# A decode kernel whose output projection is summed in 20 + 6 + 4 + 2 rows instead of 24 + 5 + 3, and whose softmax sums and attention results are gathered for two batches at a time

## The chip, the cores and the metric

The kernel runs on one core of one Trainium2 chip. The metric is device time in microseconds (us) for one execution. The time before is the median of 3 runs, 200.6 us (200.33 to 200.7). One further execution was recorded by the hardware profiler; every duration below comes from that one.

## The reference, cut to what matters

One decoding step for 8 batches (B = 8), one query each, model width D = 512:

```python
xn = layernorm(x)                                     # 8 x 512
q  = xn @ wq                                          # 32 heads of 128
k, v = the last 2048 positions of k_cache, v_cache    # 8 kv heads, each shared by 4 query heads
p  = softmax(q . k * 128**-0.5)
o  = p . v                                            # 8 x 4096
s  = o @ wo                                           # wo: 4096 x 512
h  = sigmoid(xn @ w_gate) * (xn @ w_up)               # 8 x 1792
g  = silu(h @ w_down)
y  = x + s * g
```

Nearly all bytes are keys and values: 8 batches x 8 kv heads x 2048 positions x 128 numbers in bf16 is 32 MiB for the keys and as much for the values. wo has 4 MiB, wq 4 MiB, the three gate weights 5.25 MiB.

## The kernel before, in words

**Loads.** All large loads are issued by the SP queue, in one order that the program fixes with the list `todo` (`later`, `pump`, `free`, lines 107 to 132). A load is written into the program as soon as its pool has a free buffer: five buffers of 16 KiB a partition for keys (`kpool`), four for values (`vpool`). The order is x, the gate weights, wq, then for each batch and each half of its kv heads (`i` = 0, 1) one key transfer of 2 MiB and, three steps later, one value transfer of 2 MiB. At the end come the rows of wo, which use the key buffers. `load_rows` (line 97) lays wo out so that partition p holds rows 32p to 32p + 31 of it; "row t" below means the 128 x 512 slab of the t-th of these 32 rows over all partitions (128 KiB). Line 176 cuts the 32 slabs into four transfers of 14, 10, 5 and 3 rows.

**The loop over batches** (`for b in range(B)`) is written out by hand in 16 steps for each batch; each step turns half of a key chunk with TensorE (`k_transposes`, eight 128 x 128 transposes, copied out by VectorE at line 425) and then runs the tasks put into the step. For batch b these are its scores, the softmax of batch b-1 (`row_max`, `stat_rows`, `spread_max` on ScalarE, `p_transposes`), and the values of batch b-2 (`values`, `combine`). `sums(b)` (line 516) multiplies the row sums of the exponentials, one column `st[b]`, by a 0/1 matrix in fp32, so that each output row gets its softmax denominator, and VectorE takes the reciprocal into `inv[b]`. `combine(b)` (line 547) leaves batch b's unnormalised result in `o_sb`, 128 x 128. `normalise(b)` (line 565) gathers it by an fp32 matmul with the 0/1 matrix `sel_res`, multiplies by `inv[b]` on VectorE (line 574) and reduces it into bf16 columns of `oP_sb` (line 583), from which the output projection reads. In the loop `sums` is a task of step 13 and `normalise(b - 3)` one of step 0.

The one-bank PSUM tile `m_ps` holds all small results: the maxima, the denominators (`den_ps`) and the gathered results (`oR_ps`).

**The tail**, after the last batch's keys, is straight-line code from `scores(B - 1, NU - 1)` on. It ends the softmax of batches 6 and 7 and multiplies their values. The last value transfer (batch 7, second half) is used by `some(B - 1, 1, 0, CU)`; then come `combine(7)` and `normalise(7)`.

**The output projection.** The first KS = 24 rows go into `part_ps` (line 653): matmul t writes all 512 columns to the 32 partitions of column group j = t mod 4, so four rows run side by side. The four groups' sums have then to be added. `part_ps` is copied to SBUF, the left half by ScalarE (line 665), the right half by VectorE (line 666), and `into_blocks` (line 668) adds the four groups by an fp32 matmul with the 0/1 matrix `sel_z`. `into_blocks` cuts the 512 columns into four blocks of 128 that lie on the four groups of partitions, so it takes four matmuls for a row, side by side. The last 8 rows go straight through `into_blocks` to `fin_ps`. The order on TensorE is rows 24 to 28, then `sel_z` with the copies, then rows 29 to 31. Two VectorE operations (lines 693 and 695) multiply by the gate and add x, and two transfers, one from SP and one from ScalarE's queue, write the output.

Of the kernel before, what the change touches and what calls it, by code (L numbers as in the profile page):

```python
# [10 lines left out]
def kernel(  # L11
# [13 lines left out]
    nc = tc.nc  # L25
    P = 128
    B, _, D = A_x.shape
    _, Hkv, Sk, Dh = A_k_cache.shape
# [21 lines left out]
    f32 = mybir.dt.float32  # L50
    AF = mybir.ActivationFunctionType
    ALU = mybir.AluOpType
    AX = mybir.AxisListType
# [6 lines left out]
    ktpool = ctx.enter_context(tc.tile_pool(name="ktpool", bufs=3))  # L60
# [3 lines left out]
    small = ctx.enter_context(tc.tile_pool(name="small", bufs=2))  # L64
# [39 lines left out]
    weights = {}  # L104
# [27 lines left out]
        later(tag, f)  # L132

    RT = 32
    KS = 24

    x_bf = work.tile([B, D], bf16, name="x_bf")

# [2 lines left out]
    S = Z // B  # L141
# [29 lines left out]
    for n in range(len(order) + AHEAD):  # L171
        if n < len(order):
            want_cache(k_tiles, A_k_cache, "k", *order[n])
        if n >= AHEAD:
            want_cache(v_tiles, A_v_cache, "v", *order[n - AHEAD])
    for t0, t1 in ((0, 14), (14, KS), (KS, 29), (29, RT)):
        want_rows("wo_sb", A_wo, "k", RT, t0, t1)

    pump()
# [8 lines left out]
        out=perm[:].rearrange("k (l p) -> k l p", l=G),  # L188
        in_=ident[:].rearrange("k (p l) -> k l p", l=G),
# [13 lines left out]
        out=rstd[:], in_=mv[:, 1:2], func=AF.Sqrt, bias=eps_t[:], scale=1.0  # L203
# [4 lines left out]
        out=xn_bf[:],  # L208
        in0=x_f[:],
        scalar1=mv[:, 0:1],  # L210
        scalar2=rstd[:],
        op0=ALU.subtract,
        op1=ALU.mult,
# [3 lines left out]
    for kt in range(KT):  # L217
        nc.tensor.transpose(
            out=xnT_ps[:, kt, :],
            in_=xn_bf[:].rearrange("b (p kt) -> b kt p", kt=KT)[:, kt, :],  # L220
# [11 lines left out]
    for t in p_buf:  # L232
        nc.vector.memzero(t[:])
    oP_sb = work.tile([P, RT, Z], bf16, name="oP_sb")
    nc.vector.memzero(oP_sb[:])

    NDQ = Dh // RT
    own_q = consts.tile([P, NDQ], f32, name="own_q")
    nc.vector.reduce_sum(
        out=own_q[:], in_=ident_f[:].rearrange("k (h q) -> k q h", q=NDQ), axis=AX.X  # L240
    )
    sel_z = consts.tile([P, Z], f32, name="sel_z")
    nc.vector.reduce_sum(
        out=sel_z[:], in_=ident_f[:].rearrange("k (j z) -> k z j", z=Z), axis=AX.X
# [6 lines left out]
    def hidden(name):  # L251
# [21 lines left out]
        out=h_sb[:].rearrange("k t p -> k p t"),  # L273
        in0=sig[:, :FC].rearrange("k (p t) -> k p t", t=FT),
        in1=u_ps[:].rearrange("k (p t) -> k p t", t=FT),
# [5 lines left out]
        out=hT_sb[:].rearrange("k t z -> k (t z)"),  # L281
        in_=h_sb[:].rearrange("k t p -> k (t p)"),
# [4 lines left out]
    for t in range(FT):  # L287
        j = t % NB
# [3 lines left out]
            rhs=weights[("wd_sb", t)],  # L292
# [8 lines left out]
    for j in range(NB):  # L301
# [3 lines left out]
            rhs=w_sb[:, 0, j * P : (j + 1) * P],  # L305
# [15 lines left out]
    for kt in range(KT):  # L321
        for x in range(Hkv // JQ):
            for j in range(JQ):
# [4 lines left out]
                    rhs=weights[("wq_sb", kt)][:, g * rep * Dh : (g + 1) * rep * Dh],  # L328
# [13 lines left out]
    for x in range(Hkv // JQ):  # L342
        for r in range(rep):
            nc.tensor.transpose(
                out=qT_ps[:, x, r, :], in_=q_bf[:, x, r, :], identity=ident[:]
            )
        nc.vector.tensor_copy(
            out=qm_sb[:, :, x * JQ : (x + 1) * JQ, M0 : M0 + rep],
            in_=qT_ps[:, x].rearrange("d r (j z) -> d z j r", z=Z)[:, ::S],
# [50 lines left out]
    m_ps = ps_m.tile([P, 2, 256], f32, name="m_ps", tag="m")  # L400
    r_ps = [m_ps[0:1, x, 0:P] for x in range(2)]
    nb_ps = [m_ps[:, x, 0:1] for x in range(2)]
    den_ps = [m_ps[:, x, 1:2] for x in range(2)]
    oR_ps = [m_ps[:, x, P : 2 * P] for x in range(2)]

    kT = {}
    s_ps = {}
# [1 line left out]
    st = {}  # L409
    row = {}  # L410
    inv = {}

    def k_transposes(b, u, h):
        i, j = u // NJ, u % NJ
# [58 lines left out]
    def spread_max(b):  # L473
        nc.tensor.transpose(  # L474
            out=nb_ps[b % 2],
            in_=row.pop(b)[:].rearrange("o l j h -> o (l j h)"),
            identity=ident_f[0:1, 0:1],
        )
        nb = small.tile([P, 1], f32, name="nb")
        nc.scalar.copy(out=nb[:], in_=nb_ps[b % 2])  # L480

        s = s_ps.pop(b)
        st[b] = small.tile([P, 1], f32, name="sums")
        for l in range(G):
            rows = slice(NR * l, NR * (l + 1))
            nc.scalar.activation(  # L486
                out=p_buf[b % 2][rows, :, l, :],
                in_=s[rows, :].rearrange("k (c p) -> k p c", p=PG),
                func=AF.Exp,
                bias=nb[rows, :],  # L490
                scale=scale,
                accum_out=st[b][rows, :],
            )

    def p_transposes(b, h, copy=nc.vector.tensor_copy):
# [17 lines left out]
            )  # L513


    def sums(b):
        nc.tensor.matmul(
            den_ps[b % 2],
            lhsT=sel_sum[:].rearrange("k h q -> k (h q)"),
            rhs=st.pop(b)[:],  # L520
            start=True,
            stop=True,
        )
        inv[b] = small.tile([P, 1], f32, name="inv")
        nc.vector.reciprocal(out=inv[b][:], in_=den_ps[b % 2])


    def values(b, c, tiles=range(NQ)):
# [18 lines left out]
    def combine(b):  # L547
        del pT[b]
        o_odd = small.tile([P, Dh], f32, name="o_odd")
        nc.scalar.mul(  # L550
            out=o_odd[:], in_=o_ps[:, b % 2, Dh:], mul=own_col[:, 1:2]
        )
        o = small.tile([P, Dh], f32, name="o_sb")
        nc.vector.scalar_tensor_tensor(  # L554
            out=o[:],
            in0=o_ps[:, b % 2, :Dh],
            scalar=own_col[:, 0:1],
            in1=o_odd[:],
            op0=ALU.mult,
            op1=ALU.add,  # L560
        )
        row[b] = o


    def normalise(b):
        nc.tensor.matmul(  # L566
            oR_ps[b % 2],
            lhsT=sel_res[:].rearrange("k h q -> k (h q)"),
            rhs=row.pop(b)[:],
            start=True,  # L570
            stop=True,
        )
        own = small.tile([P, NDQ, RT], f32, name="own")
        nc.vector.scalar_tensor_tensor(  # L574
            out=own[:],
            in0=oR_ps[b % 2].rearrange("p (q t) -> p q t", q=NDQ),
            scalar=inv.pop(b)[:],
            in1=own_q[:].unsqueeze(2).to_broadcast([P, NDQ, RT]),
            op0=ALU.mult,
            op1=ALU.mult,  # L580
        )
        with nc.allow_low_precision(reason="one of the addends is not zero"):
            nc.vector.reduce_sum(
                out=oP_sb[:, :, S * b],
                in_=own[:].rearrange("p q t -> p t q"),
                axis=AX.X,
            )

    for b in range(B):
        pb = b - 1 if b >= 1 else None  # L590
        pp = b - 2 if b >= 2 else None
        tasks = {s: [] for s in range(2 * NU)}
        for u in range(NU - 1):
            tasks[2 * u + 3].append(lambda u=u: scores(b, u))
        if pb is not None:
            tasks[1].append(lambda: scores(pb, NU - 1))
            tasks[2].append(lambda: row_max(pb))
            tasks[4].append(lambda: stat_rows(pb))
            tasks[6].append(lambda: spread_max(pb))
            if b < B - 1:  # L600
                tasks[11].append(lambda: p_transposes(pb, 0))
                tasks[12].append(lambda: p_transposes(pb, 1))
                tasks[13].append(lambda: sums(pb))
        if pp is not None:
            for c in range(CU):
                tasks[1 + c // 3].append(lambda c=c: values(pp, c, (0,)))
                tasks[6 + c // 3].append(lambda c=c: values(pp, c, (1,)))
            tasks[13].append(lambda: combine(pp))
        if b >= 3:
            tasks[0].append(lambda: normalise(b - 3))  # L610
        for s in range(2 * NU):
            k_transposes(b, s // 2, s % 2)
            for f in tasks[s]:
                f()
# [10 lines left out]
    spread_max(B - 1)  # L625
    p_copy(B - 2, 1, nc.vector.tensor_copy)
    some(B - 2, 0, 0, CH)
    normalise(B - 3)
    sums(B - 2)
    some(B - 2, 0, CH, CU)  # L630
    some(B - 2, 1, 0, CH)
    p_turn(B - 1, 0)
# [3 lines left out]
    some(B - 2, 1, CH, CU)  # L636
    combine(B - 2)
    some(B - 1, 0, 0, CH)
    sums(B - 1)
    some(B - 1, 0, CH, CU)  # L640
    normalise(B - 2)
    some(B - 1, 1, 0, CU)
    combine(B - 1)
    normalise(B - 1)

    fin_ps = ps_s.tile([P, P], f32, name="fin_ps", tag="s")

# [3 lines left out]
    for t in range(KS):  # L651
# [7 lines left out]
            tile_position=(0, Z * j),  # L659
            skip_group_check=True,  # L660
        )
    part = [
        ktpool.tile([P, 2, D // 2], f32, name=f"part{x}", tag="kT") for x in range(2)
    ]
    nc.scalar.copy(out=part[0][:, 0, :], in_=part_ps[:, : D // 2])
    nc.vector.tensor_copy(out=part[1][:, 0, :], in_=part_ps[:, D // 2 :])

    def into_blocks(lhsT, rhs, start, stop):
        for j in range(NB):
            nc.tensor.matmul(  # L670
                fin_ps[Z * j : Z * (j + 1), :],
                lhsT=lhsT,
                rhs=rhs(j),
                start=start,
                stop=stop,
                tile_position=(0, Z * j),
                skip_group_check=True,
            )

    for t in range(KS, RT):  # L680
        if t == 29:
            into_blocks(
                sel_z[:],
                lambda j: part[j // 2][:, 0, (j % 2) * P : (j % 2 + 1) * P],
                False,
                False,
            )
        w = weights[("wo_sb", t)]
        into_blocks(
            oP_sb[:, t, :], lambda j: w[:, j * P : (j + 1) * P], t == KS, t == RT - 1  # L690
        )
    prod = work.tile([P, P], f32, name="prod")
    nc.vector.tensor_tensor(out=prod[:], in0=gg_sb[:], in1=fin_ps[:], op=ALU.mult)  # L693
    y_bf = work.tile([P, P], bf16, name="y_bf")
# [39 lines left out]
```

## Time and profile before

| what | value |
|---|---|
| median of 3 runs | 200.6 us (200.33 to 200.7) |
| the profiled execution's own time | 201.08 us |
| its span, first to last instruction | 198.9 us |
| outside the span (201.08 - 198.9) | 2.2 us |
| TensorE busy | 156.9 us (79%) |
| VectorE busy | 122.9 us (62%) |
| ScalarE busy | 37.4 us (19%) |
| moved by the DMA engines | 81.32 MB, 409 GB/s over the span |
| mean granted TensorE clock | 0.966 |

The profiled execution is 0.48 us above the median of the runs. In the profile, PE is TensorE's matmuls, PEld its weight loads, DVE is VectorE, ACT is ScalarE, and SPq the SP queue that issues transfers. A line of the timeline has the start in us, the duration in us, engine, line of the kernel, operation, output and inputs, shape and count; in brackets stands how long the engine had been idle before and what ended the wait. fp32 matmuls appear as two instructions each.

### The profile page before, as it was taken

What the parts mean: (1) busy time and instruction counts of PE and PEld (TensorE: products, weight loads), DVE (VectorE), ACT (ScalarE), POOL (GpSimd) and SP (SyncE); (2) the same over time, 40 slices, a digit from 0 to 9 for tenths busy, and PEclk for the clock granted to TensorE, in tenths of its full rate; (3) what the DMA queues carried; (4) which work ended last, traced back from release to release, by engine and by line L of the source; (5) the groups of instructions that cost most, each with busy time, mean ns of one, the idle gap of its engine ahead of it and who ended that gap; (6) DMA issues with size and microseconds to landing.
All of it is one profiled execution on the core that took longest, in us unless ns stands there. A gap on an engine that the chain in (4) does not pass through costs nothing.

```text
span 198.9 us, 4752 instructions
## 1 busy us (share of the span) xinstructions
PE 156.9 (79%) x2130; PEld 106.7 (54%) x2130; DVE 122.9 (62%) x230; ACT 37.4 (19%) x91; POOL 1.4 (1%) x10
## 2 busy tenths in 40 slices
PE   0434457999799996999898969998988698888652
PEld 0111126777676674667565646675656565566411
DVE  4724017899798584758874947587749575742301
ACT  4101010002601500060023000600230024082000
POOL 2000000000000000000000000000000000000000
PEclk9999999999999996999999978999999999999985
DMA  5999999999999999999999999999999999999960
GB/s 212 431 435 434 435 425 428 432 428 423 435 425 432 432 425 432 425 435 425 432 432 427 425 435 428 425 430 422 438 425 435 428 425 428 432 428 430 412 263 3
DMA packets 6155, 81.32 MB, mean 409 GB/s; under 512 B 752, under 2 KB 760, under 8 KB 1272
## 3 DMA queue, kind: packets, MB, share of 16 engines
q1 hardware_dynamic: 5938, 80.10, 94.4%
q10 hardware_dynamic: 198, 0.93, 1.3%
q8 instruction: 16, 0.26, 0.5%
q14 instruction: 3, 0.02, 0.0%
HBM read 81.02 MB, written 0.01 MB: 407 GB/s over the span
## 4 chain that ended last, share of the span: by engine, by line
DMA 75%; PE 22%; SPq 1%; issue 0%; DVE 0%
DMA k_sb<-in_A_k_cache_dram 61%; PE kT_ps L420 13%; DMA wo_sb<-in_A_wo_dram 11%; PE o_ps L534 4%; PE s_ps L439 3%; DMA wg_sb<-in_B_w_gate_dram 3%; PE fin_ps L670 1%; SPq L99 1%; PE m_ps L566 0%; PE pT_ps L509 0%; DVE prod L693 0%; PE m_ps L474 0%; DVE y_bf L695 0%; PE m_ps L457 0%; SPq L89 0%
## 5 line engine op out<-in xcount | busy, mean ns | idle before, releaser
L425 DVE COPY kT_sb<-kT_ps 128x1024 bf16<-128x1024 bf16 x128 | 86.1, 687 | 34.2 <-PE kT_ps L420 33.5
L420 PE MATMUL kT_ps<-perm,k_sb 128*128 128x128 bf16 x1024 | 78.5, 225 | 11.9 <-DMA k_sb<-in_A_k_cache_dram 11.9
L420 PEld LDWEIGHTS <-k_sb 128*128 128x128 bf16 x1024 | 61.6, 101 | 31.5 <-issue 16.0
L534 PE MATMUL o_ps<-v_sb,pT_sb 128*32 128x256 bf16 x512 | 40.2, 279 | 0.9 <-DVE o_sb L554 0.9
L534 PEld LDWEIGHTS <-pT_sb 128*32 128x32 bf16 x512 | 22.1, 97 | 9.5 <-issue 3.0
L439 PE MATMUL s_ps<-kT_sb,qm_sb 128*32 128x512 bf16 x256 | 26.2, 400 | 0.7 <-DVE kT_sb L425 0.7
L486 ACT ACTIVATE p_buf<-s_ps,nb 32x512 bf16<-32x512 f32 x32 | 21.8, 680 | 0.5
L480 ACT COPY nb<-m_ps 128x1 f32<-128x1 f32 x8 | 1.3, 160 | 93.1 <-PE m_ps L474 93.1
L502 DVE COPY pT_sb<-pT_ps 128x1024 bf16<-128x1024 bf16 x14 | 9.6, 687 | 4.7 <-PE pT_ps L509 4.7
L509 PE MATMUL pT_ps<-turn_rows,p_buf 128*128 128x128 bf16 x128 | 11.0, 230 | 1.1 <-ACT p_buf L486 1.1
L509 PEld LDWEIGHTS <-p_buf 128*128 128x128 bf16 x128 | 9.3, 150 | 3.0 <-ACT p_buf L486 1.7
L439 PEld LDWEIGHTS <-qm_sb 128*32 128x32 bf16 x256 | 6.6, 93 | 7.7 <-issue 1.4
L550 ACT ACTIVATE o_odd<-o_ps,own_col 128x128 f32<-128x128 f32 x8 | 2.9, 368 | 27.2 <-PE o_ps L534 27.2
L325 PE MATMUL q_ps<-wq_sb,xnT_sb 128*32 128x512 bf16 x32 | 3.8, 627 | 4.2 <-DMA wq_sb<-in_A_wq_dram 4.2
L486 ACT ACTIVATION_READ_ACCUMULATOR p_buf<-s_ps,nb 32x1 f32 x32 | 5.9, 184 | 0.0
L454 DVE TENSOR_REDUCE st<-s_ps 128x1 f32<-128x512 f32 x8 | 5.4, 681 | 0.5 <-PE s_ps L439 0.5
L341 DVE CAST q_bf<-q_ps 128x512 bf16<-128x512 f32 x1 | 0.7, 691 | 7.4 <-PE q_ps L325 7.4
L255 PEld LDWEIGHTS <-xnT_sb 128*32 128x32 bf16 x32 | 1.2, 120 | 7.1 <-issue 6.6
L653 PE MATMUL part_ps<-wo_sb,oP_sb 128*32 128x512 bf16 x24 | 2.3, 440 | 3.0 <-DMA wo_sb<-in_A_wo_dram 3.0
L566 PE MATMUL m_ps<-o_sb,sel_res 128*128 128x128 f32 x16 | 4.0, 332 | 0.8 <-DVE o_sb L554 0.8
L325 PEld LDWEIGHTS <-xnT_sb 128*32 128x32 bf16 x32 | 1.1, 130 | 6.5 <-issue 4.7
L574 DVE SCALAR_TENSOR_TENSOR own<-m_ps,inv,own_q 128x128 f32<-128x128 f32 x8 | 2.8, 345 | 2.9 <-PE m_ps L566 2.9
(73 smaller groups left out, 62.0 us busy)
## 6 DMA issues: line engine op xcount, KB each, us to landing
k_sb<-in_A_k_cache_dram SPq DMA_DIRECT2D x16, 2048.0 KB, 33.4
v_sb<-in_A_v_cache_dram SPq DMA_DIRECT2D x16, 2048.0 KB, 29.3
wq_sb<-in_A_wq_dram SPq DMA_DIRECT2D x2, 2048.0 KB, 20.7
wu_sb<-in_B_w_up_dram SPq DMA_DIRECT2D x1, 1792.0 KB
wd_sb<-in_B_w_down_dram SPq DMA_DIRECT2D x1, 1792.0 KB
wo_sb<-in_A_wo_dram SPq DMA_DIRECT2D x1, 1792.0 KB, 18.7
wo_sb<-in_A_wo_dram SPq DMA_DIRECT2D x1, 1280.0 KB
wg_sb<-in_B_w_gate_dram ACTq DMA_DIRECT2D x1, 896.0 KB, 5.3
```

Source lines behind the costliest of these rows:

```text
L325: nc.tensor.matmul(q_ps[x][Z * j : Z * (j + 1), :], lhsT=xnT_sb[:, kt, :], rhs=weights[("wq_sb", kt)][:, g * rep * Dh : (g + 1) * rep * Dh ...
L420: nc.tensor.transpose(out=kT_ps[:, c, :], in_=k_sb[:, j * CU + h * CH + c, :], identity=perm[:],)
L425: nc.vector.tensor_copy(out=kT[(b, u)][:, h * CH : (h + 1) * CH, :], in_=kT_ps[:])
L439: nc.tensor.matmul(s_ps[b][NR * l : NR * (l + 1), :], lhsT=qm_sb[:, b, i * G + l, o : o + Z], rhs=t[:, :, PG * l : PG * (l + 1)], start=(u ...
L454: nc.vector.reduce_max(out=st[b][:], in_=s_ps[b][:], axis=AX.X)
L486: nc.scalar.activation(out=p_buf[b % 2][rows, :, l, :], in_=s[rows, :].rearrange("k (c p) -> k p c", p=PG), func=AF.Exp, bias=nb[rows, :], ...
L502: copy(out=pT[b][:, h * CH : (h + 1) * CH, :], in_=pT_ps.pop(h)[:])
L509: nc.tensor.transpose(out=pT_ps[h][:, c, :], in_=p_buf[b % 2][:, :, :, h * CH + c].rearrange("k p l -> k (p l)"), identity=turn_rows[:],)
L534: nc.tensor.matmul(o_ps[rows, b % 2, :].rearrange("k (e d) -> k e d", e=2), lhsT=pT[b][:, c, rows], rhs=v[:, m, c], start=(c == 0), stop=( ...
L550: nc.scalar.mul(out=o_odd[:], in_=o_ps[:, b % 2, Dh:], mul=own_col[:, 1:2])
L566: nc.tensor.matmul(oR_ps[b % 2], lhsT=sel_res[:].rearrange("k h q -> k (h q)"), rhs=row.pop(b)[:], start=True, stop=True,)
L574: nc.vector.scalar_tensor_tensor(out=own[:], in0=oR_ps[b % 2].rearrange("p (q t) -> p q t", q=NDQ), scalar=inv.pop(b)[:], in1=own_q[:].uns ...
```

## The change

- `KS` is 20: 20 rows are summed in column groups. The transfers of wo are five, of 12, 8, 6, 4 and 2 rows.
- `part_ps` is copied out by one ScalarE copy of 512 columns; VectorE's copy is gone.
- The `sel_z` matmuls that add the four groups come first in `fin_ps`, before row 20, instead of between rows 28 and 29.
- `sums` takes two batches' sums at once, 128 x 2. `sums_of[y]`, `inv[y]` and `o_of[y]` hold the batches 2y and 2y + 1. `sums` stands in step 13 of the odd batches only. In the tail the one for batch 6 is gone, and batch 6 is served by the one that stood there for batch 7.
- `normalise(b0, b1)` gathers one or two batches by one fp32 matmul of 128 or 256 columns. In the loop it stands in step 0 of batches 4 and 6, for two batches each. In the tail it is `normalise(4, 6)`, then batch 6 alone, then batch 7 alone. VectorE's two operations are still made for each batch.

```diff
-    KS = 24
+    KS = 20
...
-    for t0, t1 in ((0, 14), (14, KS), (KS, 29), (29, RT)):
+    for t0, t1 in ((0, 12), (12, KS), (KS, 26), (26, 30), (30, RT)):
         want_rows("wo_sb", A_wo, "k", RT, t0, t1)
...
-    den_ps = [m_ps[:, x, 1:2] for x in range(2)]
-    oR_ps = [m_ps[:, x, P : 2 * P] for x in range(2)]
+    den_ps = m_ps[:, 0, 1:3]
...
-        st[b] = small.tile([P, 1], f32, name="sums")
+        if b % 2 == 0:
+            sums_of[b // 2] = small.tile([P, 2], f32, name="sums")
...
-                accum_out=st[b][rows, :],
+                accum_out=sums_of[b // 2][rows, b % 2 : b % 2 + 1],
...
-    def sums(b):
+    def sums(y):
         nc.tensor.matmul(
-            den_ps[b % 2],
+            den_ps,
             lhsT=sel_sum[:].rearrange("k h q -> k (h q)"),
-            rhs=st.pop(b)[:],
+            rhs=sums_of.pop(y)[:],
             start=True,
             stop=True,
         )
-        inv[b] = small.tile([P, 1], f32, name="inv")
-        nc.vector.reciprocal(out=inv[b][:], in_=den_ps[b % 2])
+        inv[y] = small.tile([P, 2], f32, name="inv")
+        nc.vector.reciprocal(out=inv[y][:], in_=den_ps)
...
-    def normalise(b):
+    def normalise(b0, b1):
+        y = b0 // 2
+        x = slice(b0 % 2, (b1 - 1) % 2 + 1)
         nc.tensor.matmul(
-            oR_ps[b % 2],
+            m_ps[:, x, P : 2 * P],
             lhsT=sel_res[:].rearrange("k h q -> k (h q)"),
-            rhs=row.pop(b)[:],
+            rhs=o_of[y][:, x, :],
             start=True,
             stop=True,
         )
-        own = small.tile([P, NDQ, RT], f32, name="own")
-        nc.vector.scalar_tensor_tensor(
...
+        for b in range(b0, b1):
+            own = small.tile([P, NDQ, RT], f32, name="own")
+            nc.vector.scalar_tensor_tensor(
...
-                tasks[13].append(lambda: sums(pb))
+                if pb % 2 == 1:
+                    tasks[13].append(lambda: sums(pb // 2))
...
-        if b >= 3:
-            tasks[0].append(lambda: normalise(b - 3))
+        if b >= 4 and b % 2 == 0:
+            tasks[0].append(lambda: normalise(b - 4, b - 2))
...
-    normalise(B - 3)
-    sums(B - 2)
+    normalise(B - 4, B - 2)
...
-    sums(B - 1)
+    sums(B // 2 - 1)
     some(B - 1, 0, CH, CU)
-    normalise(B - 2)
+    normalise(B - 2, B - 1)
     some(B - 1, 1, 0, CU)
     combine(B - 1)
-    normalise(B - 1)
+    normalise(B - 1, B)
...
-    part = [
-        ktpool.tile([P, 2, D // 2], f32, name=f"part{x}", tag="kT") for x in range(2)
-    ]
-    nc.scalar.copy(out=part[0][:, 0, :], in_=part_ps[:, : D // 2])
-    nc.vector.tensor_copy(out=part[1][:, 0, :], in_=part_ps[:, D // 2 :])
+    part = ktpool.tile([P, 2, D], f32, name="part", tag="kT")
+    nc.scalar.copy(out=part[:, 0, :], in_=part_ps[:])
...
     for t in range(KS, RT):
-        if t == 29:
-            into_blocks(
-                sel_z[:],
-                lambda j: part[j // 2][:, 0, (j % 2) * P : (j % 2 + 1) * P],
-                False,
-                False,
-            )
-        w = weights[("wo_sb", t)]
-        into_blocks(
-            oP_sb[:, t, :], lambda j: w[:, j * P : (j + 1) * P], t == KS, t == RT - 1
-        )
+        if t == KS:
+            into_blocks(sel_z[:], part[:, 0, :], True, False)
+        into_blocks(oP_sb[:, t, :], weights[("wo_sb", t)], False, t == RT - 1)
```

More of the change, by code (lines that the diff above doesn't have):

```diff
@@ L411 @@
     inv = {}
+    sums_of = {}
+    o_of = {}
     def k_transposes(b, u, h):
@@ L552, in combine @@
         )
-        o = small.tile([P, Dh], f32, name="o_sb")
+        if b % 2 == 0:
+            o_of[b // 2] = small.tile([P, 2, Dh], f32, name="o_sb")
         nc.vector.scalar_tensor_tensor(
-            out=o[:],
+            out=o_of[b // 2][:, b % 2, :],
             in0=o_ps[:, b % 2, :Dh],
@@ L561, in combine @@
         )
-        row[b] = o
-    def normalise(b):
+    def normalise(b0, b1):
+        y = b0 // 2
+        x = slice(b0 % 2, (b1 - 1) % 2 + 1)
         nc.tensor.matmul(
-            oR_ps[b % 2],
+            m_ps[:, x, P : 2 * P],
             lhsT=sel_res[:].rearrange("k h q -> k (h q)"),
-            rhs=row.pop(b)[:],
+            rhs=o_of[y][:, x, :],
             start=True,
@@ L572, in normalise @@
         )
-        own = small.tile([P, NDQ, RT], f32, name="own")
-        nc.vector.scalar_tensor_tensor(
[L575 to L580, printed above, removed]
-        )
[L582 to L586, printed above, removed]
-            )
+        for b in range(b0, b1):
+            own = small.tile([P, NDQ, RT], f32, name="own")
+            nc.vector.scalar_tensor_tensor(
+                out=own[:],
+                in0=m_ps[:, b % 2, P : 2 * P].rearrange("p (q t) -> p q t", q=NDQ),
+                scalar=inv[y][:, b % 2 : b % 2 + 1],
+                in1=own_q[:].unsqueeze(2).to_broadcast([P, NDQ, RT]),
+                op0=ALU.mult,
+                op1=ALU.mult,
+            )
+            with nc.allow_low_precision(reason="one of the addends is not zero"):
+                nc.vector.reduce_sum(
+                    out=oP_sb[:, :, S * b],
+                    in_=own[:].rearrange("p q t -> p t q"),
+                    axis=AX.X,
+                )
     for b in range(B):
@@ L672, in into_blocks @@
                 lhsT=lhsT,
-                rhs=rhs(j),
+                rhs=rhs[:, j * P : (j + 1) * P],
                 start=start,
@@ L680 @@
     for t in range(KS, RT):
-        if t == 29:
-            into_blocks(
-                sel_z[:],
-                lambda j: part[j // 2][:, 0, (j % 2) * P : (j % 2 + 1) * P],
-                False,
-                False,
-            )
-        w = weights[("wo_sb", t)]
-        into_blocks(
-            oP_sb[:, t, :], lambda j: w[:, j * P : (j + 1) * P], t == KS, t == RT - 1
-        )
+        if t == KS:
+            into_blocks(sel_z[:], part[:, 0, :], True, False)
+        into_blocks(oP_sb[:, t, :], weights[("wo_sb", t)], False, t == RT - 1)
     prod = work.tile([P, P], f32, name="prod")
```

## The prediction

> **What bounds the kernel now.** First the page's slices, then what ended last, then the tail in stretches, then its timeline.
>
> ```profile
> PEclk9999999999999996999999978999999999999985
> DMA  5999999999999999999999999999999999999960
> DMA 75%; PE 22%; SPq 1%; issue 0%; DVE 0%
> k_sb<-in_A_k_cache_dram SPq DMA_DIRECT2D x16, 2048.0 KB, 33.4
> ```
>
> The transfers run at nine tenths or more from the second slice to the 38th, and three quarters of the chain that ended last are transfers. A key transfer lands 33.4 us after its issue, so SP runs far ahead: what TensorE (PE) does a few us earlier or later inside the loop moves no byte. The end is set by when the stream ends, and by what is still to do then.
>
> ```profile
> core 0: us, PE busy (x) PEld busy (x) DVE busy (x) ACT busy (x) POOL busy (x), PEclk, DMA share, GB/s
> 165.40:184.80 19.40, 17.00 (x242) 12.48 (x243) 9.47 (x19) 6.91 (x17) 0.00 (x0) 1.00 1.01 430
> 184.80:189.10 4.30, 2.46 (x35) 2.08 (x35) 1.82 (x5) 0.37 (x1) 0.00 (x0) 1.00 0.98 412
> 189.10:192.10 3.00, 1.04 (x14) 0.35 (x14) 0.00 (x0) 0.00 (x0) 0.00 (x0) 1.00 0.80 332
> 192.10:193.66 1.56, 1.25 (x10) 0.25 (x10) 0.00 (x0) 0.25 (x1) 0.00 (x0) 0.59 0.41 165
> 193.66:194.60 0.94, 0.94 (x28) 0.87 (x29) 0.42 (x1) 0.12 (x1) 0.00 (x0) 0.50 0.07 26
> ```
>
> The DMA share falls to 0.41 and 0.07 before the last rows land: most of the 16 DMA engines are done by then, and a transfer has landed only when the slowest one has. The granted clock is 0.50 from about 192.4 on.
>
> ```profile
> 184.78 1.71 PEld L534 LDWEIGHTS <-pT_sb 128*32 128x32 bf16 x32
> ...
> 188.53 0.38 DVE L583 TENSOR_REDUCE oP_sb<-own 128x32 bf16<-128x128 f32 x1
> ...
> 189.10 1.04 PE L653 MATMUL part_ps<-wo_sb,oP_sb 128*32 128x512 bf16 x14 [1.00 <-DMA wo_sb<-in_A_wo_dram]
> 192.12 1.25 PE L653 MATMUL part_ps<-wo_sb,oP_sb 128*32 128x512 bf16 x10 [1.98 <-DMA wo_sb<-in_A_wo_dram]
> ...
> 193.66 0.73 PE L670 MATMUL fin_ps<-wo_sb,oP_sb 128*32 128x128 bf16 x20 [0.29 <-DMA wo_sb<-in_A_wo_dram]
> 193.81 0.42 DVE L666 COPY part<-part_ps 128x256 f32<-128x256 f32 x1 [4.91 <-ACT part L665]
> ...
> 194.16 0.77 PE L670 MATMUL fin_ps<-part,sel_z 128*32 128x128 f32 x8
> ...
> 194.60 0.65 PE L670 MATMUL fin_ps<-wo_sb,oP_sb 128*32 128x128 bf16 x12
> 195.29 0.29 DVE L693 TENSOR_TENSOR prod<-gg_sb,fin_ps 128x128 f32<-128x128 f32 x1 [1.05 <-PE fin_ps L670]
> ```
>
> The last values start when their transfer lands, at 184.78, and the results are in `oP_sb` at 188.91. The pieces of wo then start their matmuls at 189.10, 192.12, 193.66 and 194.60. The last three rows end at 194.60 + 0.65 = 195.25; from there to the end of the span (198.9) are two VectorE operations, the output transfers and the closing code, 3.65 us that the change leaves alone.
>
> **The change part by part.**
>
> *Five transfers instead of four.* Same bytes. Five rows landed 193.66 - 192.12 = 1.54 us after the piece before, three rows 0.94 after that: two equations for a cost a piece and a cost a row, 0.30 us a row and 0.04 a piece. Test: 24 rows in two pieces from the landing at 184.78 give 7.28, and the trace has 192.12 - 184.78 = 7.34. So a fifth piece adds 0.04 us: the last row lands at 194.64. From below I exclude a gain (the bytes are the same); from above the cost of a transfer with an empty queue beside it is that of the output, issued at 195.93 and waited for until 198.0, 2.0 us. I take 0.04, because the three small pieces are the nearest rows; 2.0 stays for a rival. The Trainium skill ("DMA: Bandwidth & Descriptors", sections on the anatomy of one DMA and the rules for kernel authors) speaks against this edit: a transfer costs some 2.0 us besides its bytes, and 1 MiB or more is wanted. By that, were it paid one after the other, the end would come at 202.4. The trace disagrees for queued transfers: 0.04 us.
>
> On SP the new issue stands behind four that took 0.4 to 0.6 us each, to 172.34, and waits for the buffer of the last key tile, whose last transposes end at 172.04: no wait. Behind it SP has only the output. It is issued 22 us before it lands: nothing.
>
> Backwards from 194.64 the pieces land, with 0.04 + 0.30 n: the four rows at 194.64 - 0.64 = 194.00, the six at 192.76, the eight at 190.92, the twelve at 188.48.
>
> *Twelve and eight rows in column groups.* The twelve now wait for `oP_sb` (188.91), not for their transfer. Start about 189.0; fourteen took 1.04, so done by 190.0. The eight start at 190.92 and end by 191.97 if I take the half-clock row (ten took 1.25) and 191.5 at full clock.
>
> *One copy of 512 columns on ScalarE.* The row of the same shape (`w_sb`, line 299) took 586 ns. 191.97 + 0.04 + 0.59 = 192.60 at the latest. VectorE's copy, which began only when ScalarE's was done, goes.
>
> *`sel_z` first.* Starts at 192.65; from its start to that of the next row were 0.44 us (194.16 to 194.60), so TensorE is free at 193.09, 0.33 after the six rows landed.
>
> *Six, four, two rows.* Five rows held TensorE 0.50 us (193.66 to 194.16), so six end at 193.69, before the four land (194.00); these hold it to 194.40, before the two land at 194.64. TensorE is then idle, with its weights loaded. Eight such matmuls, begun on an idle TensorE, ended 0.41 us after their landing (the first eight of the 193.66 group). End: 195.05. Before, twelve took 0.65, behind `sel_z` in the pipeline. If the cover of 0.24 us before 194.64 were gone, each 0.1 us more would come straight on top; even a copy as long as ScalarE's of 1024 columns (1.01 us) leaves none of it on top.
>
> *Pairs.* Four `sums` matmuls (two of 0.26 us each) and four reciprocals (0.16) go; eight results take five gathers instead of eight, three of them 256 wide. A pair in one costs between one gather (0.49 us for its two instructions) and two (0.98); I take two, the nearest in columns. In the loop the DMA stream hides it: TensorE waits 11.9 us for keys. VectorE's four operations of a pair now come in one run (2 x (0.34 + 0.38) = 1.45 us), ahead of key copies in batches 4 and 6; it idles 33.5 us for key transposes, and SP's 33 us of lead hide a late buffer. In the tail the `sums` of batch 6 goes, with a wait of 0.44 us behind VectorE on `m_ps` and 0.31 us of matmul (177.23 to 177.54), and the gather beside it grows by at most 0.49: TensorE is 0.2 to 0.7 us earlier there. ScalarE's exponentials, ending at 178.74, hold the next transposes (178.98), and then the last values land at 184.78 whatever came before. The later reciprocal for batch 6 is due at 184.89 and came at 183.49 before. So nothing: between 0 and -0.7, I take 0 because the landing decides; the -0.7 stays for a rival.
>
> *Sum.* +0.04 (fifth piece) - 0.24 (0.65 to 0.41 after the last landing) + 0 (pairs) = -0.20 us. The profiled execution, 201.08, would be 200.88; it stands 0.48 above the median, so the median goes from 200.6 to **200.4**.
>
> **The rivals.**
>
> *Clock full in the tail.* The clock fell after a stretch (189.10 to 192.10) in which TensorE worked 1.04 us of 3.0. With rows starting earlier and fewer waits it may stay full. The last eight matmuls then cost 0.28 rather than 0.41: 230 ns for such a matmul (row L509 of the page) instead of 314, and half the 0.09 between starts. 200.3. For it: more work before 192; against: gaps of an us remain. The Trainium skill ("TensorE: Matmul & The Clock Gate", Part 1) says that the clock is halved after a free-running window of about 3.4 us with too little work. The trace agrees in kind: 0.50 follows the idle stretch.
>
> *The pairs were on the path.* If in unprofiled executions TensorE reaches the last values later than their landing, its up to 0.7 us count: 200.4 - 0.6 = 199.8. For it: TensorE is busy 17.0 of 19.4 us before 184.8, and its gather before the last values began only at 184.37. Against: it waited for that landing in the profiled execution, and 1 us of slack stands between `oP_sb` and the landing of the eight rows (190.0 to 190.92).
>
> *The small pieces cost a fixed time.* (The slower one.) If transfers of 2 KiB a partition no longer hide their start and completion behind the one before, the fifth adds up to 2.0 us: 202.4; from 0.24 on the kernel is slower. For it: at the very end few DMA engines work, so little lies in front of the last piece. Against: three rows landed at the same 0.30 us a row as five.
>
> *No effect.* The start at 194.60 lies 0.09 us behind the `sel_z` matmul before it, so it may have been TensorE's pace rather than the landing; the landing is then earlier and the gain larger, not smaller. I give no effect little.
>
> **How the numbers follow.** Forecast 0.61 (200.1 to 200.8 by the spread of the runs), full clock 0.11, pairs on the path 0.13, small pieces 0.12, no effect 0.03. About 0.2% (0.4 us) is what a measurement of this kernel can tell from no change; faster than 200.2 means the pairs (0.13), a part of the clock (0.04) and the lucky edge of the forecast (0.07): 0.24. Slower than 201.0: the pieces at a price above 0.6 (0.09) and the other edge (0.05): 0.14. The same 0.62. The range, 199.8 to 201.1, takes in the pairs whole and small pieces up to 0.7 us; above that about one in ten is left out.
>
> **What would show it.** Right: the last group is eight matmuls that end about 0.4 us after their start, with an idle TensorE before them; the one copy ends before 192.7; `sel_z` comes before any of rows 20 to 31; the last start moves by less than 0.1 us against the landing at 184.78. Wrong: a last start much more than 9.9 us after that landing (small pieces); last values that start more than 0.2 us after theirs, in either kernel (pairs on the path); a last group that starts straight behind the one before it (copy or `sel_z` late).

## The result

The changed kernel takes 200.04 us (median of 8 runs, 199.88 to 200.11) against 200.6 us before (8 runs, 200.33 to 200.7): a ratio of 0.9972, 95% interval 0.9962 to 0.9981. That is 0.56 us less, where 0.20 less was forecast. The profiled execution took 200.05 us with a span of 198.1.

The page's slices after:

```profile
PEclk9999999999999999999999978999999999999985
DMA  6999999999999999999999999999999999999970
DMA 76%; PE 21%; SPq 1%; issue 0%; DVE 0%
```

The transfers still run at nine tenths or more from the second slice to the 38th, and the last slices still have a low granted clock. The bound is the same; the tail is what differs. Its timeline, TensorE and the engines that feed it (start, duration, engine, line, operation, count, and the wait before it):

```profile
184.27 1.92 PE L537 MATMUL o_ps<-v_sb,pT_sb 128*32 128x256 bf16 x32 [0.27 <-DMA v_sb<-in_A_v_cache_dram]
...
187.95 0.38 DVE L589 TENSOR_REDUCE oP_sb<-own 128x32 bf16<-128x128 f32 x1
...
188.38 0.83 PE L659 MATMUL part_ps<-wo_sb,oP_sb 128*32 128x512 bf16 x12 [0.86 <-DVE oP_sb L589]
190.35 0.61 PE L659 MATMUL part_ps<-wo_sb,oP_sb 128*32 128x512 bf16 x8 [1.14 <-DMA wo_sb<-in_A_wo_dram]
...
191.02 0.59 ACT L669 COPY part<-part_ps 128x512 f32<-128x512 f32 x1 [4.42 <-PE part_ps L659]
...
191.66 0.61 PE L673 MATMUL fin_ps<-part,sel_z 128*32 128x128 f32 x8 [0.69 <-ACT part L669]
...
192.17 0.83 PE L673 MATMUL fin_ps<-wo_sb,oP_sb 128*32 128x128 bf16 x24
...
193.41 1.02 PE L673 MATMUL fin_ps<-wo_sb,oP_sb 128*32 128x128 bf16 x24 [0.41 <-DMA wo_sb<-in_A_wo_dram]
...
194.02 0.14 PEld L673 LDWEIGHTS <-oP_sb 128*32 128x32 bf16 x7 [0.19 <-issue]
194.47 0.29 DVE L688 TENSOR_TENSOR prod<-gg_sb,fin_ps 128x128 f32<-128x128 f32 x1 [6.14 <-PE fin_ps L673]
```

Two groups stand in one line from 193.41: sixteen matmuls, and eight that start at 194.02, where their weight loads resume; they end at 193.41 + 1.02 = 194.43. The pieces of eight and of four rows find TensorE idle (1.14 and 0.41 us in brackets). Before the last two rows only the weight loads stand still, for 0.19 us; by their modelled ends the matmuls before them fill the 0.61 us up to 194.02. The end comes 0.41 us after the last group starts, which is when its piece lands.

The last values start at 184.27, against 184.85 in the profile of before. That difference is not the change's: in further profiles of kernels with the old output projection they start at 184.62, 184.74 and 184.29.

### The profile page after: what moved, and what is told of

Same layout as the page of the kernel before. It is cut to its first block, busy times and chain, and to the rows that moved or that the text cites. A ratio compares the mean times of both kernels' runs of the same rounds, so it can differ in the third digit from the quotient of the medians.

```text
span 198.1 us, 4749 instructions
## 1 busy us (share of the span) xinstructions
PE 153.7 (78%) x2128; PEld 103.8 (52%) x2128; DVE 121.6 (61%) x225; ACT 37.6 (19%) x91; POOL 1.4 (1%) x10
## 4 chain that ended last, share of the span: by engine, by line
DMA 76%; PE 21%; SPq 1%; issue 0%; DVE 0%
DMA k_sb<-in_A_k_cache_dram 63%; PE kT_ps L421 12%; DMA wo_sb<-in_A_wo_dram 11%; PE o_ps L537 4%; PE s_ps L440 3%; DMA wg_sb<-in_B_w_gate_dram 2%; SPq L99 1%; PE fin_ps L673 1%; PE pT_ps L511 0%; DVE prod L688 0%; PE m_ps L475 0%; DVE y_bf L690 0%; PE m_ps L458 0%; SPq L89 0%
## 5 line engine op out<-in xcount | busy, mean ns | idle before, releaser
L421 PE MATMUL kT_ps<-perm,k_sb 128*128 128x128 bf16 x1024 | 76.9, 224 | 15.0 <-DMA k_sb<-in_A_k_cache_dram 15.0
L421 PEld LDWEIGHTS <-k_sb 128*128 128x128 bf16 x1024 | 60.1, 100 | 35.2 <-DMA k_sb<-in_A_k_cache_dram 18.1
L558 DVE SCALAR_TENSOR_TENSOR o_sb<-o_ps,own_col,o_odd 128x128 f32<-128x128 f32 x8 | 2.7, 340 | 3.1 <-ACT o_odd L553 3.1
L325 PEld LDWEIGHTS <-xnT_sb 128*32 128x32 bf16 x32 | 1.1, 130 | 6.4 <-issue 4.7
L255 PE MATMUL h_ps<-wu_sb,xnT_sb 128*32 128x448 bf16 x16 | 1.7, 572 | 3.3 <-DMA wu_sb<-in_B_w_up_dram 3.3
```

Of the source, the lines that this page charges most:

```text
L325: nc.tensor.matmul(q_ps[x][Z * j : Z * (j + 1), :], lhsT=xnT_sb[:, kt, :], rhs=weights[("wq_sb", kt)][:, g * rep * Dh : (g + 1) * rep * Dh ...
L421: nc.tensor.transpose(out=kT_ps[:, c, :], in_=k_sb[:, j * CU + h * CH + c, :], identity=perm[:],)
L558: nc.vector.scalar_tensor_tensor(out=o_of[b // 2][:, b % 2, :], in0=o_ps[:, b % 2, :Dh], scalar=own_col[:, 0:1], in1=o_odd[:], op0=ALU.mul ...
```

## The experiments

Each was timed in five rounds beside the kernel before on the same chip. Since every timed run also has its span, mean spans are given too; for the kernel before they scatter less than the times (standard deviation 0.12 to 0.18 us against 0.24 to 0.25). The kernel before had a mean span of 198.78 on the chip of the first four (27 runs), 198.64 on that of the next four (35) and 198.75 on that of the last four (23).

**1. The kernel before, again.**

> The kernel before, unchanged, for a second profile of it and for the noise. Every theory: 1.000 of before within 0.001. What it tells apart is in its profile: the first one was 0.48 us above the median of its runs. If only that execution was slow, the last values land here at about 184.3 instead of 184.78 and the span is 198.3 to 198.5; if the stream of the kernel before always ends that late, they land at 184.8 again.

Measured: ratio 1.0005 (0.9993 to 1.0016). The span was 198.9 again and the last values started at 184.62, so the first profile was no unusual execution. The last landing came earlier than in it, and the end did not. Timeline of this second profile of the kernel before (weight loads left out):

```profile
191.90 1.47 PE L653 MATMUL part_ps<-wo_sb,oP_sb 128*32 128x512 bf16 x10 [1.36 <-DMA wo_sb<-in_A_wo_dram]
193.40 0.37 ACT L665 COPY part<-part_ps 128x256 f32<-128x256 f32 x1 [6.45 <-PE part_ps L653]
193.45 0.72 PE L670 MATMUL fin_ps<-wo_sb,oP_sb 128*32 128x128 bf16 x20
193.80 0.42 DVE L666 COPY part<-part_ps 128x256 f32<-128x256 f32 x1 [5.12 <-ACT part L665]
193.95 0.76 PE L670 MATMUL fin_ps<-part,sel_z 128*32 128x128 f32 x6
194.38 0.43 PE L670 MATMUL fin_ps<-wo_sb,oP_sb 128*32 128x128 bf16 x4
194.49 0.43 PE L670 MATMUL fin_ps<-part,sel_z 128*32 128x128 f32 x2
194.59 0.65 PE L670 MATMUL fin_ps<-wo_sb,oP_sb 128*32 128x128 bf16 x8
195.28 0.29 DVE L693 TENSOR_TENSOR prod<-gg_sb,fin_ps 128x128 f32<-128x128 f32 x1 [1.06 <-PE fin_ps L670]
```

The last rows are released at 194.38 but run in among `sel_z` matmuls that had to wait for VectorE's copy (to 194.22), and end at 195.24, 0.86 us after the landing. The ten rows before the copies took 1.47 us here and 1.25 in the first profile. The reason is in the stretches of this execution (busy times of the engines, granted clock in the third column from the right):

```profile
188.90:191.90 3.00, 1.64 (x16) 0.41 (x15) 0.00 (x0) 0.00 (x0) 0.00 (x0) 0.54 0.81 337
191.90:193.40 1.50, 1.46 (x10) 0.30 (x9) 0.00 (x0) 0.00 (x1) 0.00 (x0) 0.50 0.52 214
```

The granted clock is already halved in the first of them, where it was 1.00 in the first profile.

**2. The output projection alone.** KS = 20, the five pieces, one copy, `sel_z` first; `sums` and `normalise` stay as before.

```diff
-    KS = 24
+    KS = 20
...
-    for t0, t1 in ((0, 14), (14, KS), (KS, 29), (29, RT)):
+    for t0, t1 in ((0, 12), (12, KS), (KS, 26), (26, 30), (30, RT)):
...
-        if t == 29:
...
+        if t == KS:
...
```

> The change's output projection alone (20 rows in column groups, pieces of 12, 8, 6, 4 and 2 rows, one copy, sel_z first), with sums and results gathered batch by batch as before. Theory A (the forecast: only the last group of matmuls counts, and the pairs nothing): -0.20 us, so about 200.4, and the rest of the measured -0.56 us is noise that comes back in no part. Theory B (the pairs were on the path): -0.20 us here, and -0.36 in the pairs alone. Theory C (the tail is worth more than forecast): -0.5 to -0.6 us here.

Measured: 0.9968 (0.9956 to 0.9981), 0.64 us; mean span 198.36, 0.42 less than before. The whole gain is here, within the noise, and it is more than 0.20: theory C.

**3. The pairs alone.** `sums(y)`, `normalise(b0, b1)` and their places as in the change; the output projection as before.

> The pairs alone (sums and results of two batches by one fp32 matmul), with the output projection of the kernel before (24 rows, pieces of 14, 10, 5 and 3). Theory A: 0.0 us. Theory B: -0.36 us. Theory C: 0.0 us. If the pairs shorten the stream itself, the last values land earlier against the start of the stream than in the kernel before; if they only bring TensorE earlier, the landing stays and the start of the last values moves.

Measured: 0.9997 (0.9988 to 1.0006); mean span 198.83 against 198.78. The pairs are worth nothing that can be measured: at most 0.24 us by the interval. Theory B, which asked for 0.36 and was also a rival of the prediction, falls.

**4. The last two pieces as one.**

```diff
-    for t0, t1 in ((0, 12), (12, KS), (KS, 26), (26, 30), (30, RT)):
+    for t0, t1 in ((0, 12), (12, KS), (KS, 26), (26, RT)):
```

> The changed kernel with its last two pieces, of 4 and 2 rows, as one of 6 rows (pieces 12, 8, 6, 6). Forecast's own step: one transfer less (-0.04 us), but 24 matmuls instead of 8 after the last landing, 0.83 instead of 0.41 us: +0.38 us against the changed kernel, about 200.4. If the last group is not what sets the end, 0.0.

Measured: 0.9996 (0.9987 to 1.0006), so the gain of the change is gone; mean span 198.77. That is 0.08 us below the kernel before, where the forecast's step left about 0.2. Its timeline:

```profile
194.36 0.83 PE L673 MATMUL fin_ps<-wo_sb,oP_sb 128*32 128x128 bf16 x24 [0.63 <-DMA wo_sb<-in_A_wo_dram]
...
195.24 0.29 DVE L688 TENSOR_TENSOR prod<-gg_sb,fin_ps 128x128 f32<-128x128 f32 x1 [6.55 <-PE fin_ps L673]
```

Six rows after the last landing take the 0.83 us that were forecast. With one copy and `sel_z` first, what sets the end is the last landing plus the last group.

After these, a second thing had to be told apart. The profiles of the kernels with five transfers of wo had shorter closings: less time from the output's issue to the end of the span, and less outside the span.

**5. Five transfers in the kernel before.**

```diff
-    for t0, t1 in ((0, 14), (14, KS), (KS, 29), (29, RT)):
+    for t0, t1 in ((0, 14), (14, KS), (KS, 29), (29, 31), (31, RT)):
```

> The kernel before with its last piece of 3 rows cut into 2 and 1, so five transfers of wo, and nothing else changed. Seen so far: kernels with five transfers of wo (changed kernel, output projection alone) take 1.97 us outside their span and 2.96 us from the output's issue to the span's end, those with four (kernel before twice, pairs alone, last six) 2.14 to 2.17 and 3.01 to 3.03. Theory R (one more load in the queue shortens the closing of the program): -0.20 to -0.25 us here. Theory G (the whole gain is in TensorE's last group of matmuls): 0.0 us, since the end follows VectorE's copy by 1.0 us in both.

Measured: 0.9990 (0.9981 to 0.9999), 0.20 us; mean span 198.54, 0.10 less, and outside the span 2.00 us in the mean against 2.09. The time is what theory R gave, though the interval reaches almost to nothing. In its profile the end still follows VectorE's copy (193.98) by 1.02 us.

**6. Four transfers in the changed kernel.**

```diff
-    KS = 20
+    KS = 16
...
-    for t0, t1 in ((0, 12), (12, KS), (KS, 26), (26, 30), (30, RT)):
+    for t0, t1 in ((0, KS), (KS, 26), (26, 30), (30, RT)):
```

> The changed kernel with its first two pieces as one: 16 rows in column groups, pieces of 16, 10, 4 and 2. The last group stays two rows on an idle TensorE, but wo has four transfers. Theory R: 0.20 us slower than the changed kernel, that is -0.40 us against the kernel before (ratio 0.998), with 2.15 us outside the span. Theory G: as the changed kernel or 0.04 faster (ratio 0.997), with 1.97 us outside the span.

Measured: 0.9979 (0.9968 to 0.9989); mean span 198.17, 0.47 less than before, and 2.19 us outside the span. The time is what theory R gave, but its profiled execution had 1.79 us outside the span and others up to 2.9: single executions scatter too much for the sign that the expectation named. What holds is the span: the last group's gain comes without a fifth transfer.

**7. One more load, elsewhere.** x is loaded a second time at the start, into a tile that nobody reads.

```diff
+    x_2 = work.tile([B, D], bf16, name="x_2")
...
         q0.dma_start(out=x_bf[:], in_=A_x.flatten_outer_dims())
+        q0.dma_start(out=x_2[:], in_=A_x.flatten_outer_dims())
```

> The kernel before with x loaded a second time at the start, 8 KB on the SP queue into a tile that nobody reads; wo in four transfers as before. Theory R: -0.2 us, with 1.97 us outside the span and 2.96 from the output's issue to the end. If only the fifth transfer of wo does it, or nothing: 0.0 us, up to +0.05 for the load.

Measured: 0.9997 (0.9988 to 1.0005); mean span 198.65 against 198.64, outside 2.05. The output's issue to the end took 2.96 us in its profile, as with five pieces, instead of 3.01, so those 0.05 us go with the number of loads. The time outside the span moved by 0.05 where theory R asked for 0.12, and the median by 0.05 where it asked for 0.2. That speaks against theory R but does not exclude it, since 0.2 us less still lies in the interval.

**8. The kernel before without copies and `sel_z`.** The sums of the first 24 rows are left out of the result.

```diff
...
-    nc.scalar.copy(out=part[0][:, 0, :], in_=part_ps[:, : D // 2])
-    nc.vector.tensor_copy(out=part[1][:, 0, :], in_=part_ps[:, D // 2 :])
...
-        if t == 29:
-            into_blocks(
-                sel_z[:],
...
```

> The kernel before without the two copies of part_ps and the sel_z matmuls; the first 24 rows' sums are left out of the result. If the last landing sets the end, as the forecast had it: the last twelve matmuls then find an idle TensorE, -0.1 us. If VectorE's copy sets the end (in both profiles of the kernel before the end lies 1.01 us after that copy, though the last landing differs by 0.22): the end falls to 0.52 us after the last landing, -0.3 us in an execution such as the second profile, -0.13 in one such as the first.

Measured: 0.9987 (0.9977 to 0.9996), 0.26 us; mean span 198.36 against 198.64, 0.28 less. Timeline (weight loads left out):

```profile
191.48 1.46 PE L653 MATMUL part_ps<-wo_sb,oP_sb 128*32 128x512 bf16 x10 [2.00 <-DMA wo_sb<-in_A_wo_dram]
193.01 0.72 PE L664 MATMUL fin_ps<-wo_sb,oP_sb 128*32 128x128 bf16 x20
193.94 0.51 PE L664 MATMUL fin_ps<-wo_sb,oP_sb 128*32 128x128 bf16 x12 [0.21 <-DMA wo_sb<-in_A_wo_dram]
```

The same twelve matmuls now wait for their landing and end 0.51 us after it, although the ten rows ran as slowly as in run 1. So in the kernel before the copies and `sel_z` together set the end, not the last landing. Which of them it is, this run does not say.

**9. One copy in the kernel before.**

```diff
...
-    nc.scalar.copy(out=part[0][:, 0, :], in_=part_ps[:, : D // 2])
-    nc.vector.tensor_copy(out=part[1][:, 0, :], in_=part_ps[:, D // 2 :])
...
+    nc.scalar.copy(out=part[:, 0, :], in_=part_ps[:])
...
```

> The kernel before with one ScalarE copy of 512 columns in place of the two halves; nothing else. If VectorE's copy sets the end of the kernel before: ScalarE's copy takes 0.59 us and ends 0.24 us before VectorE's would (0.37 + 0.03 + 0.43 = 0.83), so the end comes 0.15 to 0.24 us sooner, where the last landing takes over. If the last landing sets the end: 0.0.

Measured: 0.9994 (0.9985 to 1.0003), which by itself decides nothing; mean span 198.58 against 198.75, 0.17 less, as the copy theory gave. In its profile the one copy takes 0.59 us, and the last twelve matmuls start at 194.19 and end 0.55 later:

```profile
193.12 0.59 ACT L663 COPY part<-part_ps 128x512 f32<-128x512 f32 x1 [6.44 <-PE part_ps L653]
...
193.76 0.65 PE L667 MATMUL fin_ps<-part,sel_z 128*32 128x128 f32 x8
...
194.19 0.55 PE L667 MATMUL fin_ps<-wo_sb,oP_sb 128*32 128x128 bf16 x12
```

That is the part of run 8's gain that belongs to VectorE's copy. `sel_z` moved to the front without any other edit was not run.

**10 and 11. A last piece of one row.**

```diff
-    for t0, t1 in ((0, 12), (12, KS), (KS, 26), (26, 30), (30, RT)):
+    for t0, t1 in ((0, 12), (12, KS), (KS, 28), (28, 31), (31, RT)):
```

> The changed kernel with pieces of 12, 8, 8, 3 and 1 rows: four matmuls after the last landing instead of eight. If the end is the last landing plus the last group: 0.29 instead of 0.41 us after it, -0.1 us against the changed kernel, -0.5 against the kernel before. If the group before it is not done in time: 0.0 to +0.1.

Run 11 has KS = 16 and pieces of 16, 8, 5, 2 and 1.

> The changed kernel with 16 rows in column groups and pieces of 16, 8, 5, 2 and 1. By the same step as the run with a last piece of one row: -0.1 us against the changed kernel. If the smaller first sum is worth something by itself, because the copy and sel_z are done earlier, it is faster than that run; by the forecast it is not, since TensorE is idle before the last landing in both.

Measured: 0.9964 (0.9952 to 0.9976) and 0.9963 (0.9951 to 0.9975); mean spans 198.26 and 198.12 against 198.75. The changed kernel had 0.9972 and a mean span of 198.14. The 0.1 us can't be told from the noise; neither is shown to beat the changed kernel.

**12. The kernel before with TensorE kept at work.**

```diff
+    warm_ps = ps_t.tile([P, D], f32, name="warm_ps", tag="t")
...
+        if t == 14:
+            for _ in range(8):
+                nc.tensor.matmul(
+                    warm_ps[:],
+                    lhsT=ident[:],
+                    rhs=weights[("wo_sb", 0)],
+                    start=True,
+                    stop=True,
+                )
```

> The kernel before with eight further matmuls of 512 columns into a PSUM tile that nobody reads, between its first 14 rows and the landing of the next ten, so that TensorE has work there. If the half clock after the idle stretch is what lets the copies, sel_z and the last rows come late: the clock stays at 1.00 through the ten rows, these end about 0.3 us sooner and so does the end, -0.2 to -0.35 us, down to the last landing. If the clock has no part: 0.0; if the extra matmuls run at half clock and are late themselves: slower by up to 0.5.

Measured: 1.0011 (0.9991 to 1.0030), but the executions fall into two groups: five with a span of 198.0 to 198.3 and seven with 199.1 to 199.6. The profile is of the first group. Its stretches (columns as in run 1) and timeline:

```profile
188.40:191.50 3.10, 2.82 (x21) 1.17 (x23) 0.00 (x0) 0.00 (x0) 0.00 (x0) 1.00 0.88 366
191.50:193.03 1.53, 0.83 (x11) 0.23 (x10) 0.25 (x1) 0.37 (x1) 0.00 (x0) 1.00 0.51 211
```

```profile
191.51 0.82 PE L663 MATMUL part_ps<-wo_sb,oP_sb 128*32 128x512 bf16 x10 [0.17 <-DMA wo_sb<-in_A_wo_dram]
...
192.78 0.42 DVE L676 COPY part<-part_ps 128x256 f32<-128x256 f32 x1 [4.49 <-ACT part L675]
...
193.95 0.35 PE L680 MATMUL fin_ps<-wo_sb,oP_sb 128*32 128x128 bf16 x12 [0.24 <-DMA wo_sb<-in_A_wo_dram]
```

At full clock the ten rows take 0.82 us, VectorE's copy is done at 193.20, and even twelve matmuls end 0.35 us after the last landing. The spans of this group have a mean of 198.12, as short as the changed kernel's (198.14). The two groups lie 0.63 us below and 0.58 us above the kernel before in span, both more than expected (0.35 and 0.5), so the clock may not be all of it. That the other group had the half clock while its extra matmuls ran, and that these were late, was not seen, since no profile of such an execution was taken. The mean granted clocks of whole executions, 0.981 to 0.991 in the first group and 0.983 to 0.991 in the other, do not tell them apart.

## Why the prediction was right or wrong

The direction and the place were right, and the size was too small: -0.20 us forecast, -0.56 measured (0.38 to 0.76 by the interval). That 200.04 still lies in the stated range is luck in part. The range reached down to 199.8 for the pairs, and below 200.2 the prediction counted on the pairs, on a full clock or on the edge of the scatter; the pairs gave nothing and the clock was halved.

*What sets the end* is the step that failed. The prediction put it as "The last three rows end at 194.60 + 0.65 = 195.25" and counted from the last landing. In the kernel before, the end follows VectorE's copy instead. In the five profiles with both copies at half clock the end lies 1.01 or 1.02 us after that copy: 194.24 to 195.25, 194.22 to 195.24, and the same in the pairs alone (194.12 to 195.14), with five transfers (193.98 to 195.00) and with the extra load (193.90 to 194.92). From the last landing it is 0.65 in the first profile and 0.86 in the second. In all five the last rows start 0.43 or 0.44 us behind the start of `sel_z`, as they also do in run 9, so that start shows TensorE's pace as well. In the first profile landing and pace met at 194.60. The paragraph on no effect read that coincidence rightly ("the landing is then earlier and the gain larger"), yet the sum took the first profile's 0.65 as the kernel's value.

*The mis-sized term* is therefore the 0.24; it measured about 0.38. The copies and `sel_z` are worth 0.28 us of span (run 8). Twelve matmuls after the landing took 0.51 there and eight take 0.41 in the changed kernel, 0.10 more. With 0.05 for the closing the sum is 0.43. The output projection alone measured 0.42 (five runs, standard deviation 0.24, so the close agreement is partly luck), and run 6, without the shorter closing, 0.47.

*Why the copy comes late* was read as a possible gain of the changed kernel (the rival of a full clock), but it is a cost of the kernel before. With the clock halved throughout, the ten rows take 1.47 us, with the clock halved for part of them 1.25, at full clock 0.82 (run 12). The Trainium skill ("TensorE: Matmul & The Clock Gate", Part 1) says that the window over which work is counted runs freely. The profiles fit that: the clock was granted in full until about 192.4 in one execution of the same kernel and halved through most of 188.90 to 191.90 (0.54) in another. In the new order such a loss is covered: in run 2 the eight rows took 1.04 us instead of the changed kernel's 0.61, the copy ended at 192.14 instead of 191.61, and the last group still took 0.41 us (194.24 to 194.65).

*The rest of the 0.56*, some 0.13 us, is not placed, and 0.43 lies within the interval by itself. Part of it may lie outside the span: 1.87 us in the mean for the changed kernel, 2.08 to 2.09 for the kernel before in the three sets of runs beside the experiments. For the eight runs of the kernel before in the result the spans are not on record, so their 200.6 us can't be split. The five kernels with five transfers of wo have means of 1.86 to 2.00 outside the span, those with four 2.05 to 2.19. The prediction left this time alone, as it did the closing. Run 7 speaks against the mere number of loads. The cause stays open.

*What held.* The fifth transfer costs next to nothing: from the start of the last values to that of the last group are 9.75 us in both profiles (184.85 to 194.60, 184.27 to 194.02; forecast +0.04; the prediction's 184.78 is the start of their weight loads). The fixed 2.0 us for a transfer did not appear, so the rival of small pieces falls. The Trainium skill ("DMA: Bandwidth & Descriptors", section on the anatomy of one DMA) fits that figure to transfers issued from GpSimd, while these are issued by SP. The rows of the last four pieces started 6.08, 7.90, 9.14 and 9.75 us after the last values; forecast were landings 6.14, 7.98, 9.22 and 9.86 after theirs. The twelve rows waited for `oP_sb`; the copy took 0.59 and ended at 191.61; `sel_z` came before row 20; the weight loads stood still for 0.19 us before the last landing (forecast: TensorE idle for 0.24), though the matmuls in flight filled that time; the last eight matmuls took 0.41. The pairs were worth nothing measurable (run 3): in the profile of the changed kernel TensorE waits 0.27 us for the last value transfer. The clock did not stay full: 0.50 from 192.17 on.

## What to carry to other kernels

Where two things release the same instruction within a few hundredths of a us in one profile, work out what each gives by itself before taking either for the bound: an end at a constant distance from one of them in a second profile points to the bound, and a run without that work tests it. Put the work that needs a PSUM copy and a second pass as early as its inputs allow, and keep for the end only the least that must follow the last landing. In a tail that waits for transfers, cost matmuls at half clock and at full clock; which one an execution gets can differ.

## What was not expected of the hardware

- The granted clock fell at different places of the same tail in different executions, and the kernel with extra matmuls had executions of two kinds, with spans of 198.0 to 198.3 and 199.1 to 199.6 us.
- In the profiles with one transfer more on the SP queue, be it a fifth piece of wo or a second load of x, the time from the output's issue to the end of the span was 2.95 to 2.96 us; in the others it was 3.01 to 3.03.
- Outside the span the kernels with five transfers of wo took 1.86 to 2.00 us in the mean, the others 2.05 to 2.19; nothing in the traces shows why.
